# Sigmoid attention and a gated layer on one core: four pairs of 448-token blocks, and the second half of the output layer by seven products

## The chip, the cores and the metric

The kernel runs on one core of one Trainium2 chip. Its time is the device time of one launch in microseconds (us). Before the change the median of three runs is 1235.81 us (1235.44 to 1236.19). A core has a matrix engine (TensorE, "PE" in the profile, with its weight loads shown apart as "PEld"), a vector engine (DVE), a scalar engine (ACT), GpSimd (POOL) and a queue of transfers (SP, "SPq"). Each engine takes its own instructions strictly in the order of the program and waits on semaphores for the others.

## The reference

There are two stages. Sigmoid attention with 8 batches, 12 heads, 448 tokens and a head size of 64, then a gated layer over all 3584 tokens with a model width of 768 and d_ff of 1536:

```
scores = scale * q @ k.T - log(S)
x      = sigmoid(scores) @ v                    # -> 3584 x 768
gate   = sigmoid(x @ w_gate)                    # 768 -> 1536
val    = x @ w_val                              # 768 -> 1536
out    = (gate * val) @ w_out                   # 1536 -> 768
```

q, k and v arrive as 32-bit floats, the three weight matrices as 64-bit floats.

## The kernel before, in words

Attention comes first. It runs over 24 groups of four heads (three groups to a batch) in seven steps each, and it writes x, transposed, to DRAM: six tensors of 128 model rows by 3584 tokens. Beside it, DVE and POOL turn the 64-bit words of the first half of the weights into 32-bit floats (`convert`).

The gated layer works with hidden columns in blocks of 128, taken in pairs `jp`; six pairs in two sets of three. A visit is one set with one group of tokens, and a visit has two parts. In the *units* the hidden values of the three pairs are made: for each pair one unit for the gate (sigmoid on ACT) and one for the value, which is multiplied into the gate. In the *output stage* the hidden values are multiplied with `w_out`. The first set leaves its partial results in DRAM (`part`), the second adds them and writes the result.

Every matrix product is exact to about 32 bits by splitting each operand into a high part (rounded to the format that TensorE takes in one pass) and a low part (the rest). One product of 128x128 weights with a moving tile is thus three matmuls: low weights with high data, high with low, high with high. So every moving tile needs a cast (ACT) and a subtraction (DVE) before it can be used.

A unit works on two hidden blocks times two token blocks at once. It takes seven products in place of eight (Winograd's form of Strassen's scheme), of nine matmuls each: three of the six 128-row slices of x, times three. The sums and differences of the weights are made once by `convert` and lie in DRAM as seven operands (`ad`, loaded into the ring `A` on SP, one per product). The sums of x, in place on POOL, with their casts and low parts are made by `split_x` once per visit. DVE, POOL and ACT add the seven results up to the four blocks (`p1`, `p5`, `u2`, `u3`, `u4`, `c22`, `c`). Work that follows a result is put into a list `later` and is issued after the next product, so that an engine's queue does not stand still for it.

The tokens are seven blocks of 512. Six form three pairs. Block 0 stays alone (`alone`): it takes the ordinary eight block products, two of them per accumulation. The output stage takes the ordinary form throughout: for each of the six output tiles `o` and each token block 18 (first set or second) matmuls, over three pairs, two hidden blocks and three terms; its weights `wo` come through a second ring. The list `visits` sets the order: the first set with block 0 and with the three pairs, then the second set with the last pair, the two others and block 0.

The order in each engine's queue is the order of the Python code. PSUM has eight banks: four for the units (`un`) and four for the output stage (`mm`).

Of the kernel before, what the change touches and what calls it, by code (L numbers as in the profile page):

```python
# [18 lines left out]
P = 128  # L19
# [5 lines left out]
T = 512  # L25

SET = 3
# [7 lines left out]
RING = 6  # L35
RING_OUT = 6
# [3 lines left out]
def sigmoid_attention_glu_kernel(ctx: ExitStack, tc: tile.TileContext, qk, v, wg, wv, wo, out):  # L40
# [22 lines left out]
    NB = B * S // T  # L63
# [9 lines left out]
    N_OPS, A21 = 7, 7  # L73
# [8 lines left out]
    part = [[dram.tile([P, T], F32, name=f"part{b}_{o}") for o in range(NO)] for b in range(NB)]  # L82
    a_dram = [[[dram.tile([P, 2, CW], F32, name=f"ad{jp}_{t}_{n}") for n in range(N_OPS + 1)] for t in range(2)]
              for jp in range(NJ // 2)]
    o_dram = [dram.tile([NO, P, 2, 2, P], F32, name=f"od{jp}") for jp in range(NJ // 2)]


    def chunks(jps):
        res = []
        for jp in jps:  # L90
            for w in (wg, wv, wo):
                res += [w[2 * jp + j][:, c * CW:(c + 1) * CW] for j in range(2) for c in range(2)]
        return res
# [36 lines left out]
    def convert(words, jps):  # L130
# [25 lines left out]
        def to_o(jp, j, c):  # L156
            return lambda hl: [dict(out=o_dram[jp][c * KC:(c + 1) * KC, :, j, n].rearrange("o p f -> p o f"),
                                    in_=hl[:, n].rearrange("p (o f) -> p o f", f=P)) for n in range(2)]

        def chunk(tag, sends):  # L160
            f = pool.tile([P, CW], F32, tag=tag, name="wf", bufs=1)
            words.first(f)
            split(1)
            send(1)
            yield f
            send(0)
            split(0)
            words.second()
            high(f, sends)
            yield f  # L170

        for jp in jps:
            for t in range(2):
                fs = []
                for i, n in enumerate((0, 4, A21, 6)):
                    for f in chunk(f"wf{i}", to_a(jp, t, n)):
                        yield
                    fs.append(f)
                a11, a12, a21, a22 = fs
                split(0)  # L180

                s2 = pool.tile([P, CW], F32, tag="wf4", name="wf", bufs=1)
                for n, (to, x, y, op) in enumerate(((a22, a21, a22, ALU.add), (s2, a22, a11, ALU.subtract),
                                                    (a21, a11, a21, ALU.subtract), (a12, a12, s2, ALU.subtract))):
                    split(1)
                    send(1)
                    nc.gpsimd.tensor_tensor(out=to, in0=x, in1=y, op=op)
                    high(to, to_a(jp, t, (1, 2, 3, 5)[n]))
                    yield
            for j in range(2):  # L190
                for c in range(2):
                    for _ in chunk(f"wf{2 * j + c}", to_o(jp, j, c)):
                        yield
# [6 lines left out]
    SUMS = ("p1", "p5", "u2", "u3", "u4", "c22", "g0", "g1", "g2", "g3", "c0", "c1")  # L200

    def sb(tag):
        return xpool.tile([P, T], F32, tag=tag, name=tag)
# [4 lines left out]
    def load_x(blocks):  # L208

        order = [(i, k) for k in range(KC) for i in range(4)] if len(blocks) == 2 else [(2 * c, k) for c in range(2) for k in range(KC)]  # L210
        for tag, (i, k) in zip(SUMS, order):
            x = sb(tag)
            nc.sync.dma_start(out=x, in_=x_dram[i // 2 * KC + k][:, blocks[i % 2] * T:blocks[i % 2] * T + T])
            xs[i, k] = x
            yield

    def split_x(blocks, cast=nc.scalar.copy):

        sums = {1: (0, 1, 0), 2: (0, 3, 0), 3: (1, 3, 1), 6: (0, 2, 0)} if len(blocks) == 2 else {}
        use = dict(enumerate((0, 0, 0, 1, 2, 3, 0))) if len(blocks) == 2 else {5: 0, 6: 2}  # L220
        for n, i in use.items():
            for k in range(KC):
                if n in sums:
                    to, x, y = sums[n]
                    nc.gpsimd.tensor_tensor(out=xs[to, k], in0=xs[x, k], in1=xs[y, k], op=ALU.subtract)  # L225
                x = xs[i, k]
                hi = xpool.tile([P, T], F32R, tag=f"bh{n}{k}", name="bh")
                lo = xpool.tile([P, T], F32R, tag=f"bl{n}{k}", name="bl")
                cast(hi, x)
                yield  # L230
                nc.vector.tensor_tensor(out=lo, in0=x, in1=hi, op=ALU.subtract)
                bs[n, k] = hi, lo


    wanted = [(jp, t, n) for s, bl in visits for jp in sets[s] for t in range(2)
              for n in (range(N_OPS) if len(bl) == 2 else (0, 4, A21, 6))]
    ring, wos = [], {}

    def load_operand():
        if wanted:  # L240
            jp, t, n = wanted.pop(0)
            ring.append(xpool.tile([P, 2, KC, P], F32R, tag="A", name="A", bufs=RING))
# [12 lines left out]
    with tc.manual_schedule(), tc.tile_pool(name="att", bufs=2) as att, tc.tile_pool(name="sc", bufs=2, space=PSUM) as scp, \  # L255
# [122 lines left out]
        for _ in range(RING_OUT):  # L378
            load_out()
# [241 lines left out]
```

## Time and profile before

| what | us |
|---|---|
| median of three runs | 1235.81 |
| own time of the profiled execution | 1237.49 |
| its span | 1235.3 |
| attention, to the first matmul of the gated layer | 259.3 |
| TensorE busy | 1217.5 |
| DVE, ACT, POOL busy | 658.8, 417.9, 402.2 |

The profile's page shows busy time by engine, the chain of work that ended last, and groups of instructions by line. Rows of the timeline give the start in us from the span's start, the duration in us, the engine, the line, the operation, output and inputs, and in brackets the idle time of the engine just before and what ended it. A matmul's row is longer than the distance to the next one, since matmuls overlap in the array: the distance of starts is what counts. Rows of the windows view give the busy time of each engine in a stretch of time, the granted clock of TensorE as a share of full speed, the share of the 16 DMA engines that was busy, and the rate in GB/s. Rows of the waits view give total us, times and the longest. Rows of the DMA view give the count, KB of one, and the median time from issue to landing.

### The profile page before, as it was taken

The numbers are of one execution on the slowest core, as the hardware profiler recorded it, in microseconds if no ns is written. First come the engines' busy times: TensorE is split into PE (matmuls) and PEld (weight loads), VectorE is DVE, ScalarE is ACT, GpSimd is POOL, SyncE is SP. The second block draws the span as 40 slices with busy tenths as digits, with TensorE's granted clock in tenths as the row PEclk, the third lists the DMA queues.
The fourth block names the chain that finished last, engine by engine and source line by source line (L and its number), as shares of the span: only waits on it lengthen the run. The fifth ranks groups of instructions, "written<-read, shape, count | busy, mean of one in ns | idle before, by whom it ended". The sixth has DMA issues, their size and how long they took to land.

```text
span 1235.3 us, 19057 instructions
## 1 busy us (share of the span) xinstructions
PE 1217.5 (99%) x6916; PEld 902.9 (73%) x6916; DVE 658.8 (53%) x1073; ACT 417.9 (34%) x610; POOL 402.2 (33%) x418
## 2 busy tenths in 40 slices
PE   9999999999799999999999999999999999999998
PEld 3333444468588888887888788888888888888886
DVE  5666677626748867688777601336444452442111
ACT  6777777732312233322412112222222221221010
POOL 2323423304535365534736300235122342220000
PEclk9999999999899999999999999999999999999999
DMA  9999999889699988999788756668766776667745
GB/s 319 327 344 345 357 340 330 296 294 369 228 300 297 281 303 279 299 297 335 259 292 284 231 170 205 193 194 304 233 200 192 267 248 216 194 202 254 226 142 188
DMA packets 150045, 328.43 MB, mean 266 GB/s; under 512 B 15296, under 2 KB 40000, under 8 KB 149952
## 3 DMA queue, kind: packets, MB, share of 16 engines
q1 hardware_dynamic: 149952, 327.22, 79.4%
q8 instruction: 55, 0.90, 0.3%
q14 instruction: 38, 0.31, 0.1%
HBM read 246.94 MB, written 80.22 MB: 265 GB/s over the span
## 4 chain that ended last, share of the span: by engine, by line
PE 93%; DMA 3%; DVE 2%; POOL 1%; ACT 0%; issue 0%; SPq 0%; POOLq 0%; DVEq 0%; ACTq 0%
PE un L401 42%; PE acc L503 26%; PE sc L279 9%; PE av L296 9%; PE un L461 7%; DMA ad<-whl 1%; DMA A<-ad 1%; DMA xd<-x 0%; DVE hl L485 0%; DMA wo<-od 0%; PE sc L334 0%; DVE whl L140 0%; POOL g L225 0%; DVE wf L126 0%; DVE x L313 0%
## 5 line engine op out<-in xcount | busy, mean ns | idle before, releaser
L401 PE MATMUL un<-bh,A 128*128 128x512 f32 x1512 | 466.4, 389 | 0.0
L401 PEld LDWEIGHTS un<-bh,A 128*128 128x128 f32 x1512 | 283.8, 188 | 58.7
L503 PE MATMUL acc<-hh,wo 128*128 128x512 f32 x1008 | 314.4, 391 | 1.6 <-DMA wo<-od 1.0
L401 PE MATMUL un<-bl,A 128*128 128x512 f32 x756 | 294.1, 389 | 0.0
L503 PEld LDWEIGHTS acc<-hh,wo 128*128 128x128 f32 x1008 | 190.1, 189 | 43.2 <-DMA wo<-od 2.1
L503 PE MATMUL acc<-hl,wo 128*128 128x512 f32 x504 | 197.6, 392 | 8.7 <-DVE hl L485 8.7
L282 ACT ACTIVATE a<-sc,bias 128x896 f32<-128x896 f32 x168 | 169.2, 1008 | 67.0 <-PE sc L279 63.3
L401 PEld LDWEIGHTS un<-bl,A 128*128 128x128 f32 x756 | 141.9, 188 | 29.6
L279 PE MATMUL sc<-qk 64*64 64x448 f32 x1344 | 159.7, 541 | 0.5 <-ACT a L282 0.5
L296 PE MATMUL av<-a,v 64*64 64x448 f32 x1344 | 158.3, 536 | 0.0
L150 POOL CAST whl<-wf 128x384 fp32r<-128x384 f32 x120 | 72.5, 605 | 263.4 <-DVE wf L128 209.2
L414 POOL TENSOR_TENSOR u<-u,p 128x512 f32<-128x512 f32 x36 | 47.7, 1325 | 274.9 <-DVE u L414 274.5
L503 PEld LDWEIGHTS acc<-hl,wo 128*128 128x128 f32 x504 | 95.0, 189 | 30.3 <-DVE hl L485 10.7
L279 PEld LDWEIGHTS sc<-qk 64*64 64x64 f32 x1344 | 55.7, 134 | 73.4 <-issue 60.1
L414 DVE TENSOR_TENSOR u<-un,p 128x512 f32<-128x512 f32 x36 | 24.8, 689 | 157.1 <-PE un L401 157.1
L296 PEld LDWEIGHTS av<-a,v 64*64 64x64 f32 x1344 | 55.6, 133 | 70.7 <-issue 70.1
L484 ACT CAST hh<-g 128x512 fp32r<-128x512 f32 x72 | 42.2, 621 | 191.2 <-DVE g L481 142.7
L448 ACT ACTIVATE g<-c 128x512 f32<-128x512 f32 x72 | 43.1, 628 | 153.1 <-DVE c L414 149.0
L461 PE MATMUL un<-bh,A 128*128 128x512 f32 x288 | 89.4, 390 | 1.8 <-DMA A<-ad 1.8
L140 DVE TENSOR_TENSOR whl<-wf,whl 128x384 fp32r<-128x384 f32 x120 | 82.6, 692 | 8.3 <-POOL whl L150 8.2
L414 DVE TENSOR_TENSOR ob<-acc,pb 128x512 f32<-128x512 f32 x42 | 29.0, 691 | 93.3 <-PE acc L503 88.2
L115 POOL TENSOR_SCALAR wf<-wf 128x384 f32<-128x384 f32 x72 | 43.5, 604 | 84.5 <-DVE wf L114 52.8
(53 smaller groups left out, 1128.7 us busy)
## 6 DMA issues: line engine op xcount, KB each, us to landing
A<-ad SPq DMA_DIRECT2D x300, 384.0 KB, 3.8
ad<-whl SPq DMA_DIRECT2D x96, 384.0 KB, 5.8
wo<-od SPq DMA_DIRECT2D x144, 256.0 KB, 4.0
qk<-qk SPq DMA_DIRECT2D x23, 896.0 KB, 6.9
v<-vv SPq DMA_DIRECT2D x24, 448.0 KB, 6.1
xd<-x SPq DMA_DIRECT2D x48, 224.0 KB, 5.9
part<-ob SPq DMA_DIRECT2D x42, 256.0 KB, 3.5
pb<-part SPq DMA_DIRECT2D x42, 256.0 KB, 3.8
```

What stands on the lines that cost most here:

```text
L115: nc.gpsimd.tensor_scalar(out=f, in0=f, scalar1=F32_MAX, scalar2=F64_ZERO, op0=ALU.min, op1=ALU.max)
L140: nc.vector.tensor_tensor(out=hl[:, 1], in0=to, in1=hl[:, 0], op=ALU.subtract)
L150: nc.gpsimd.tensor_copy(hl[:, 0], to)
L279: nc.tensor.matmul(sc[halves[u], h, :S], lhsT=qkt[halves[h], p, k0:k0 + HP], rhs=qkt[halves[h], p, :S], start=True, stop=True)
L282: nc.scalar.activation(a, sc[:, :, :S], AF.Sigmoid, bias=bias, scale=scale)
L296: nc.tensor.matmul(avs[key][halves[h], :S], lhsT=vt[halves[u], g, h], rhs=a[halves[u], h], start=start, stop=g == last)
L401: nc.tensor.matmul(acc, lhsT=w, rhs=m, start=i == 0, stop=i == len(terms) - 1)
L414: engine.tensor_tensor(out=to, in0=x, in1=y, op=ALU.add)
L448: nc.scalar.activation(gates[i], acc, AF.Sigmoid)
L461: nc.tensor.matmul(acc, lhsT=w, rhs=m, start=i == 0, stop=i == len(terms) - 1)
L484: nc.scalar.copy(hh, g)
L503: nc.tensor.matmul(acc, lhsT=w, rhs=m, start=i == 0 and some[0] == 0, stop=i == len(terms) - 1 and some[-1] == SET - 1)
```

## The change

Tokens are now eight blocks of 448, one batch each, in four pairs; `alone` is gone, and every unit uses the seven products. There are eight visits: the first set with pairs 0 to 3, then the second set with pairs 3, 0, 1, 2. The x of pair 0 is loaded and split during attention, for seven operands of three slices (before: the two halves of block 0, six slices), by POOL casts.

In the second set, the output stage takes the seven products too. The "weights" are then a pair of output tiles (`o` and `o + 3`) by a pair of hidden blocks, the moving side is a pair of hidden blocks by a pair of token blocks, and the three pairs `jp` of the set are added in PSUM: three pairs times three terms, nine matmuls to a product. The sums of `w_out` are made by `convert` (`oo` in DRAM; 36 steps to a pair in place of 32) and come through the same ring `A`. The sums, casts and low parts of the hidden values are made in `hidden_operands`. The partial results of the first set are added on POOL (`partial`). The units and output products of the second set share eight PSUM banks (`us`).

Besides, the last two of the three terms of a product trade places (high weights with high data comes before high weights with low data), `split_x` issues sum, cast and low part of one slice in three successive steps, a corner of the weights that no product uses is not written to DRAM any more, and both rings have eight places in place of six.

```diff
-    pairs = [(b, b + 1) for b in range(1, NB, 2)]
-    visits = [(0, bl) for bl in [(0,)] + pairs] + [(1, bl) for bl in pairs[-1:] + pairs[:-1] + [(0,)]]
+    pairs = list(range(B // 2))
+    visits = [(0, pr) for pr in pairs] + [(1, pr) for pr in pairs[-1:] + pairs[:-1]]
...
+    def product(pool, operands, dims="p (a k f) -> p a k f"):
+
+        acc = pool.tile([P, 512], F32, tag="un", name="un")[:, :S]
+        a = ring.pop(0).rearrange(dims, a=2, f=P)
+        terms = []
+        for k, (hi, lo) in enumerate(operands):
+            w = (a[:, 0, k], a[:, 1, k]) if dims.startswith("p (a") else (a[:, k, 0], a[:, k, 1])
+            terms += [(w[1], hi), (w[0], hi), (w[0], lo)]
...
+    with tc.manual_schedule(), tc.tile_pool(name="fs", bufs=1, reuse_waits="tile") as fs, \
+            tc.tile_pool(name="us", bufs=8, space=PSUM, reuse_waits="tile") as us:
...
+        def hidden_operands(slot):
...
+            def value(i, acc):
+                gated(i, acc)
+                b[i] = gates[i]
+                if i == 0:
+                    high(0)
+                    later.append(lambda: low(0))
+                elif i == 3:
+                    later.append(lambda: (high(5), later.append(lambda: low(5))))
+                elif i == 1:
+                    total(1)
+                    total(3)
+                    later.append(lambda: (high(1), low(1), high(3), low(3), total(2)))
+                else:
+                    high(4)
+                    later.append(lambda: (high(2), low(2), low(4), total(6), later.append(lambda: (high(6), low(6)))))
...
+            def step():
+                nonlocal steps
+                steps += 1
+                send_due(steps)
+                for _ in range(2):
+                    next(x_loads, None)
+                if steps > 2:
+                    next(splits, None)
+                if steps % 4 == 0:
+                    next(splits, None)
+
+            for o in range(KC):
...
+                nc.scalar.copy(p1, out_product(0))
+                nc.scalar.copy(p5, out_product(1))
+                plus(u2, out_product(2), p1)
+                plus(u4, u2, p5, nc.gpsimd)
+                partial(p1, p1, 0, 0)
+                partial(u4, u4, 0, 1)
+                plus(u3, out_product(3), u2)
+                plus(p5, u3, p5, nc.gpsimd)
+                ob = result()
+                partial(ob, p5, 1, 1)
+                partial(u3, u3, 1, 0)
+                send(1, 1, ob, 3)
+                for n, x, m, t in ((4, p1, 0, 0), (5, u4, 0, 1), (6, u3, 1, 0)):
+                    ob = result()
+                    plus(ob, out_product(n), x)
+                    send(m, t, ob)
+                load_part(o + 1)
```

How the change moves instructions is shown at the first output stage of the second set, for DVE first. In the rows, `g0` to `g3` are the four blocks gate times value of the last pair, `hh` and `hl` their high and low parts, `c0` and `c1` sums out of PSUM, `ou`, `op` and `ob` tiles of the output stage; the numbers tell buffers apart. Before, from the last unit's fifth product on:

```order
L414 TENSOR_TENSOR c1_9515<-un_9516,p1_9455 128x512
L481 TENSOR_TENSOR g0_9419<-c1_9515,g0_9419 128x512
L485 TENSOR_TENSOR hl_9530<-g0_9419,hh_9529 128x512
L414 TENSOR_TENSOR c0_9533<-un_9534,u4_9459 128x512
L414 TENSOR_TENSOR c1_9554<-un_9555,u3_9458 128x512
L481 TENSOR_TENSOR g2_9453<-c1_9554,g2_9453 128x512
L485 TENSOR_TENSOR hl_9548<-g3_9434,hh_9547 128x512
L485 TENSOR_TENSOR hl_9552<-g1_9437,hh_9551 128x512
L485 TENSOR_TENSOR hl_9571<-g2_9453,hh_9570 128x512
L414 TENSOR_TENSOR ob_9633<-acc_9598,pb_8877 128x512
```

And with the change, from the same product on:

```order
L408 TENSOR_TENSOR c1_9019<-un_9020,p1_8959 128x448
L465 TENSOR_TENSOR g0_8923<-c1_9019,g0_8923 128x448
L225 TENSOR_TENSOR hl_9035<-g0_8923,hh_9034 128x448
L408 TENSOR_TENSOR c0_9037<-un_9038,u4_8963 128x448
L225 TENSOR_TENSOR hl_9073<-g0_8923,hh_9072 128x448
L225 TENSOR_TENSOR hl_9077<-g1_8941,hh_9076 128x448
L408 TENSOR_TENSOR c1_9056<-un_9057,u3_8962 128x448
L465 TENSOR_TENSOR g2_8957<-c1_9056,g2_8957 128x448
L225 TENSOR_TENSOR hl_9070<-g3_8938,hh_9069 128x448
L225 TENSOR_TENSOR hl_9105<-g0_8923,hh_9104 128x448
L225 TENSOR_TENSOR hl_9084<-g2_8957,hh_9083 128x448
L225 TENSOR_TENSOR hl_9128<-g0_8923,hh_9127 128x448
```

There are seven low parts in place of four, and two of them (of `g0` and `g1` after the first sums) stand ahead of the sum of the unit's last product, `c1_9056`.

On ACT, at the same place, before:

```order
L484 CAST hh_9529<-g0_9419 128x512
L484 CAST hh_9547<-g3_9434 128x512
L484 CAST hh_9551<-g1_9437 128x512
L484 CAST hh_9570<-g2_9453 128x512
L229 CAST bh_9637<-p1_9574 128x512
```

And with the change:

```order
L584 CAST hh_9034<-g0_8923 128x448
L584 CAST hh_9069<-g3_8938 128x448
L584 CAST hh_9072<-g0_8923 128x448
L584 CAST hh_9076<-g1_8941 128x448
L584 CAST hh_9083<-g2_8957 128x448
L584 CAST hh_9104<-g0_8923 128x448
L664 COPY op1_9086<-un_9091 128x448
L584 CAST hh_9127<-g0_8923 128x448
```

The high part of the third operand, `hh_9104`, stands behind that of `g2`, `hh_9083`.

On POOL, from the last unit's fourth product on, before:

```order
L414 TENSOR_TENSOR c22_9460<-u3_9458,p5_9456 128x512
L481 TENSOR_TENSOR g3_9434<-c22_9460,g3_9434 128x512
L481 TENSOR_TENSOR g1_9437<-c0_9533,g1_9437 128x512
L225 TENSOR_TENSOR p1_9574<-p5_9576,p1_9574 128x512
L225 TENSOR_TENSOR u4_9582<-c22_9584,u4_9582 128x512
```

And with the change:

```order
L408 TENSOR_TENSOR c22_8964<-u3_8962,p5_8960 128x448
L465 TENSOR_TENSOR g3_8938<-c22_8964,g3_8938 128x448
L465 TENSOR_TENSOR g1_8941<-c0_9037,g1_8941 128x448
L225 TENSOR_TENSOR g0_8923<-g1_8941,g0_8923 128x448
L225 TENSOR_TENSOR g1_8941<-g3_8938,g1_8941 128x448
L225 TENSOR_TENSOR g0_8923<-g3_8938,g0_8923 128x448
L225 TENSOR_TENSOR g0_8923<-g2_8957,g0_8923 128x448
L408 TENSOR_TENSOR ou4_9090<-ou2_9088,op5_9087 128x448
L408 TENSOR_TENSOR op1_9086<-op1_9086,pb_8345 128x448
L408 TENSOR_TENSOR ou4_9090<-ou4_9090,pb_8347 128x448
L408 TENSOR_TENSOR op5_9087<-ou3_9089,op5_9087 128x448
L408 TENSOR_TENSOR ob_9181<-op5_9087,pb_8351 128x448
```

Four sums of the hidden values come in, and the six sums of each output step; the sums of the next pair's x (`p1_9574<-p5_9576,p1_9574` before) come behind them.

More of the change, by code (lines that the diff above doesn't have):

```diff
@@ L377, in sigmoid_attention_glu_kernel, with after, run_later, plus @@
             pass
-        for _ in range(RING_OUT):
-            load_out()
+    later = []
+    def after():
+        for f in list(later):
+            later.remove(f)
+            f()
+    def run_later():
+        while later:
+            later.pop(0)()
+    def plus(to, x, y, engine=nc.vector):
+        engine.tensor_tensor(out=to, in0=x, in1=y, op=ALU.add)
+    cs = itertools.cycle(("c0", "c1"))
+    def product(pool, operands, dims="p (a k f) -> p a k f"):
[5 more added lines that the diff above has]
+            terms += [(w[1], hi), (w[0], hi), (w[0], lo)]
+        for i, (w, m) in enumerate(terms):
+            nc.tensor.matmul(acc, lhsT=w, rhs=m, start=i == 0, stop=i == len(terms) - 1)
+        load_operand()
+        after()
+        return acc
+    def unit(pool, tick, done):
+        def next_product(n):
+            return product(pool, [bs[n, k] for k in range(KC)])
+        p1, p5, u2, u3, u4, c22 = (sb(n) for n in SUMS[:6])
+        nc.scalar.copy(p1, next_product(0))
+        tick()
+        nc.scalar.copy(p5, next_product(1))
+        tick()
+        plus(u2, next_product(2), p1)
+        plus(u4, u2, p5, nc.gpsimd)
+        tick()
+        plus(u3, next_product(3), u2)
+        plus(c22, u3, p5, nc.gpsimd)
+        tick()
+        c = sb(next(cs))
+        plus(c, next_product(4), p1)
+        done(0, c)
+        later.append(lambda: done(3, c22))
+        tick()
+        c = sb(next(cs))
+        plus(c, next_product(5), u4)
+        done(1, c)
+        tick()
+        c = sb(next(cs))
+        plus(c, next_product(6), u3)
+        done(2, c)
+        tick()
+    gates = {}
+    def gate(i, acc):
+        gates[i] = sb(f"g{i}")
+        nc.scalar.activation(gates[i], acc, AF.Sigmoid)
+    def gated(i, acc):
+        engine = nc.vector if i in (0, 2) else nc.gpsimd
+        engine.tensor_tensor(out=gates[i], in0=acc, in1=gates[i], op=ALU.mult)
+        return engine
     with tc.manual_schedule(), tc.tile_pool(name="ff", bufs=1, reuse_waits="tile") as ff, \
@@ L468, in gate_alone, with load_out @@
-        def gate_alone(i, acc):
-            gates[i] = ff.tile([P, T], F32, tag="ob", name="ob", bufs=3)
-            nc.scalar.activation(gates[i], acc, AF.Sigmoid)
-        def hidden(slot, products):
+        wanted_out = [(jp, o) for _ in pairs for o in range(NO) for jp in sets[0]]
+        def load_out():
+            if wanted_out:
+                jp, o = wanted_out.pop(0)
+                wos[jp, o] = ff.tile([P, 2, 2, P], F32R, tag="wo", name="wo", bufs=RING_OUT)
+                nc.sync.dma_start(out=wos[jp, o].bitcast(F32), in_=o_dram[jp][o])
@@ L474, in hidden @@
+        for _ in range(RING_OUT):
+            load_out()
+        def hidden(slot, tick):
             hs = {}
             def value(i, acc):
-                g = gates[i]
-                hh = ff.tile([P, T], F32R, tag=f"hh{slot}{i}", name="hh")
-                hl = ff.tile([P, T], F32R, tag=f"hl{slot}{i}", name="hl")
-                engine = nc.vector if products is alone or i in (0, 2) else nc.gpsimd
-                engine.tensor_tensor(out=g, in0=acc, in1=g, op=ALU.mult)
+                engine = gated(i, acc)
+                hs[i] = tuple(ff.tile([P, S], F32R, tag=f"h{a}{slot}{i}", name=f"h{a}") for a in "hl")
```

351 lines of the change are left out of this document (159 added, 192 removed).

## The prediction

> **What bounds the kernel now.** I read the busy times first, then the chain of waits, then TensorE's own waits. Page and chain:
>
> ```profile
> span 1235.3 us, 19057 instructions
> PE 1217.5 (99%) x6916; PEld 902.9 (73%) x6916; DVE 658.8 (53%) x1073; ACT 417.9 (34%) x610; POOL 402.2 (33%) x418
> PE 93%; DMA 3%; DVE 2%; POOL 1%; ACT 0%; issue 0%; SPq 0%; POOLq 0%; DVEq 0%; ACTq 0%
> 257.05 2.25 PE av L296 x24
> 259.30 7.93 PE un L461 x34
> 752.70 85.68 PE un L401 x378
> 838.38 49.01 PE acc L503 x216
> 1218.89 12.55 PE acc L503 x54
> ```
>
> TensorE is busy for 99% of the span and makes 93% of the chain. The gated layer starts at 259.3 and its matmuls end at 1218.89 + 12.55 = 1231.4. The chain's unbroken pieces give the price of one matmul, start to start: 85.68 / 378 = 0.2267 us, and 49.01 / 216 the same. The groups by line give the count (a row of high data each; the low data make half as many again):
>
> ```profile
> L401 PE MATMUL un<-bh,A 128*128 128x512 f32 x1512 | 466.4, 389 | 0.0
> L503 PE MATMUL acc<-hh,wo 128*128 128x512 f32 x1008 | 314.4, 391 | 1.6 <-DMA wo<-od 1.0 <-ACT hh L484 0.5
> L461 PE MATMUL un<-bh,A 128*128 128x512 f32 x288 | 89.4, 390 | 1.8 <-DMA A<-ad 1.8
> ```
>
> 1.5 x (1512 + 1008 + 288) = 4212 matmuls, times 0.2267 = 954.9 us. So the profiled span is 259.3 + 954.9 + 17.2 of waits and slow clock + 3.9 after the last matmul = 1235.3. The median of the runs, 1235.81, is 0.5 above this span. TensorE's waits:
>
> ```profile
> PE acc L503 <- DVE hl L485: 8.7, 4, 4.9
> PE un L461 <- DMA A<-ad: 1.8, 1, 1.8
> PE acc L503 <- DMA wo<-od: 1.0, 1, 1.0
> 324.53 0.80 PE L503 MATMUL acc<-hl,wo 128*128 128x512 f32 x1 [4.94 <-DVE hl L485]
> 326.40 1.06 PE L503 MATMUL acc<-hh,wo 128*128 128x512 f32 x2
> 327.25 0.63 PE L503 MATMUL acc<-hl,wo 128*128 128x512 f32 x1
> ```
>
> Nearly all are output stages that start before the low parts of the last hidden values are there; and after the 4.94 us wait matmuls stand (327.25 - 326.40) / 2 = 0.425 us apart, at half the clock.
>
> **The matmuls.** Now all up products go by sevens: 4 pairs x 6 hidden pairs x 2 x 7 x 9 = 3024. The first set's output: 8 blocks x 6 tiles x 18 = 864. The second set's: 4 pairs x 3 x 7 x 9 = 756. In sum 4644 in place of 4212, each with 448 columns in place of 512. Columns fall from 2,156,544 to 2,080,512, by 3.5%. What matters is whether a 448-column matmul really is shorter. Streaming 512 columns at half the clock takes 0.425 us, so about 0.213 at the full clock, and some 0.0133 of the 0.2267 is overhead. If it is fixed, 448 columns take 0.1867 + 0.0133 = 0.2000; if all is in proportion, 0.1983. From the other side the weight load could forbid any gain, 0.2267. These rows tell how near that is:
>
> ```profile
> 332.31 0.19 PEld L503 LDWEIGHTS acc<-hh,wo 128*128 128x128 f32 x1 [0.33 <-DMA wo<-od]
> 332.42 0.19 PEld L503 LDWEIGHTS acc<-hl,wo 128*128 128x128 f32 x1
> 332.65 0.42 PEld L503 LDWEIGHTS acc<-hh,wo 128*128 128x128 f32 x2
> ```
>
> A load takes 0.19 us in the records, but after a wait the next one starts 0.11 later: the array has taken the first by then. 0.11 is well under 0.20, and even 0.19 is. I take 0.2000: 4644 x 0.2000 = 928.8 us, 26.1 less.
>
> The Trainium skill, "TensorE: Matmul & The Clock Gate", section "Back-to-back issue gap", gives N / 2.4 GHz plus 2.5 ns. That is 216 ns for 512 columns where this trace has 227, so its constant is too small here; with the constant taken as fixed, its sum would fall by the same 26.7 ns per matmul.
>
> **Attention.** It loses six slices of early splitting and gains 21, with 12 sums on POOL.
>
> ```profile
> 0.00:259.30 259.30, 257.40 (x2705) 112.09 (x2705) 162.82 (x330) 190.19 (x216) 83.03 (x130) 1.00 0.94 328
> ```
>
> DVE (162.8 of 259.3) and POOL (83.0) have room for some 10 and 22 us more; ACT, which feeds TensorE here, gets nothing. Nothing in this stage moves: 0. If DVE came late with the sums that free the PSUM tiles of `av`, the price would be a few us; that is in the range.
>
> **First set, four output stages.** The 4.9 us wait came from the early splits of the next pair, pushed through at the end of the first visit; they are gone. The three others together had 8.7 - 4.9 = 3.8. The cover before the third hidden pair's terms is 24 matmuls, now 4.8 us in place of 5.4, while `convert`'s steps (108 in place of 96 over a shorter time) keep their length in the same queue. I take 3.8 / 3 = 1.25 for each of four: 5 us (0 to 8).
>
> **Second set, four output stages: a new wait.** This is how such a transition runs now; DVE and POOL from the timeline, ACT's cast from the groups:
>
> ```profile
> 969.02 0.69 DVE L414 TENSOR_TENSOR c<-un,p 128x512 f32<-128x512 f32 x1 [1.29 <-PE un L401]
> 969.75 1.26 DVE L481 TENSOR_TENSOR g<-c,g 128x512 f32<-128x512 f32 x1
> 971.69 0.69 DVE L485 TENSOR_TENSOR hl<-g,hh 128x512 fp32r<-128x512 f32 x1 [0.69 <-ACT hh L484]
> 972.30 1.49 DVE L414 TENSOR_TENSOR c<-un,u 128x512 f32<-128x512 f32 x2
> 973.83 1.08 DVE L481 TENSOR_TENSOR g<-c,g 128x512 f32<-128x512 f32 x1
> 973.07 1.29 POOL L481 TENSOR_TENSOR g<-c,g 128x512 f32<-128x512 f32 x1 [2.60 <-DVE c L414]
> L484 ACT CAST hh<-g 128x512 fp32r<-128x512 f32 x72 | 42.2, 621 | 191.2 <-DVE g L481 142.7
> ```
>
> The output stage began at 973.07, just when POOL could start block `g1`. With 7/8 of the columns I use 1.13 for POOL, 0.60 for DVE (0.95 where it writes `g`), 0.55 for a cast, and count from the start of the output stage. POOL: `g1` to 1.1, first sum to 2.3, second to 3.4. ACT: cast of the first sum to 2.8; DVE: its low part to 3.4 or 3.5. ACT: cast of the second to 3.95; DVE: its low part to 4.6. Only then comes the sum of the unit's last product on DVE, to 5.2, and block `g2`, to 6.1. POOL's third sum is done at about 4.8, but its cast stands on ACT behind that of `g2`: 6.1 + 0.55, then 0.55, is 7.2, and its low part is there at 7.8. TensorE wants these in the third product, after 2 x 9 matmuls and six more: 4.8 for the high part, 5.2 for the low. It waits 2.4 and then 0.2: 2.6 us. The second product needs its parts at 3.0 and 3.4, and has them at 2.8 and 3.5; the later ones are in time. Four visits: 10.4 us. Below, POOL and DVE run unhindered in another order of events and it is 6; above, with DVE and POOL slowed by each other, 3.5 each and half clock behind it, 18. Behind the waiting matmul stand all others; only the PSUM results that DVE still owes gain time.
>
> **Second set, the rest of its output stages.** Each lasts 21 x 1.8 = 37.8 us, and three of four also load and split the next pair. Three things could run late:
>
> ```profile
> A<-ad SPq DMA_DIRECT2D x300, 384.0 KB, 3.8
> 285.00:300.00 15.00, 15.00 (x68) 12.43 (x67) 9.32 (x17) 3.40 (x6) 3.44 (x4) 1.00 1.04 402
> L225 POOL TENSOR_TENSOR g<-c,g 128x512 f32<-128x512 f32 x15 | 22.5, 1498 | 1.3 <-DVE bl L231 1.3
> 994.94 1.75 POOL L225 TENSOR_TENSOR g<-c,g 128x512 f32<-128x512 f32 x1
> 995.46 1.78 DVE L231 TENSOR_TENSOR bl<-g,bh 128x512 fp32r<-128x512 f32 x1
> ```
>
> Transfers: 21 operands of 393 kB and 32 tiles of 229 kB are 15.6 MB, 413 GB/s, and the queues have moved 402. They end 1 us late, and the ring runs eight products, 14.4 us, ahead of a latency of 3.8. POOL: 18 sums of results and 12 of x are 30 x 1.13 = 34 us, or 39 at 1498 x 7/8 = 1.31 us, for 37.8 + 2.6. Nine of the sums of x fall into the middle third, where POOL gets some 5 us late. SP then waits for POOL's result ahead of the next loads, and DVE with it. Eight PSUM banks (14.4 us) and the ring cover that. I take 1 us in all; uncovered it is some 5 us in each of three stages.
>
> The last visit has no next pair. Behind its last matmul stand as before one DVE sum and one transfer: 3.9. The first operands come with two more places in the ring and without the early loads of x beside them: 0.5 in place of 1.8.
>
> **Sum.** 259.3 + 928.8 + (0.5 + 5 + 10.4 + 1 = 16.9) + 3.9 = 1208.9, and 0.5 to the median: 1209 us. The gain is nearly all columns; the waits come out as long as before, in other places.
>
> **The rivals.**
>
> *A matmul does not get shorter with its columns* (slower). If the loads of weights, 0.19 us in every record, need more than the 0.20 us between starts, spacing stops falling. The point from which this decides is (1235.3 - 259.3 - 3.9 - 16.9) / 4644 = 0.2057 us. With no gain at all, 4644 x 0.2267 = 1052.8 and the time is 1333; half way, 0.2133, it is 1271. For it: all matmuls of this shape in the trace have 512 columns, so no row shows a shorter one. Against it: 0.11 between loads after the wait. 0.10.
>
> *POOL becomes the bound of the output stages.* The last two rows above overlap and both last far longer than the 1.29 and 0.69 of others like them: POOL and DVE hinder each other when both read two tiles of SBUF. If POOL's 30 sums and DVE's 21 low parts went one after another, 34 + 21 x 0.60 = 46.6 us, 6 over 40.4. Three stages: 18 us, 1227. Against it: eight banks and the ring give more than 6 us of cover, and the x splits may end within the next units. 0.12. The Trainium skill, "SBUF — State Buffer", section "Who interferes with whom", has this as an exclusive lock: a DVE instruction with two SBUF inputs and a GpSimd one that reads SBUF go one after the other. The two rows agree in kind (1.75 and 1.78).
>
> *Everything hides:* 0.1983 a matmul (920.9) and half the waits, 8.4: 259.3 + 920.9 + 8.4 + 3.9 + 0.5 = 1193. 0.10.
>
> **How the numbers follow.** The forecast has 0.68, with a range of its own of 1195 to 1222 (the waits' bounds, and 0.1983). The range for 8 in 10 takes in part of the two rivals at its ends: 1192 to 1232. A difference of 0.2%, 2.5 us, is about what can be told from none. Faster by more: forecast, "everything hides" and most of "POOL", 0.86. Within it: 0.03, the edge of POOL and a spacing close to 0.2057. Slower: 0.11, the first rival and a remainder.
>
> **What would show it.** In the new profile: pieces of 378 matmuls in the chain of 75.6 us (0.2000); attention's end at 259 to 260; in TensorE's waits four of 2 to 3 us on the cast or the low part of the hidden values, in the third product of each of the second set's output stages; POOL near full there; no wait for operands after the first visit. The forecast is wrong if spacing is over 0.203, if TensorE waits for PSUM, x or operands in the second set, or if attention ends later than 262.

## The result and the profile after

The change made the kernel slower: 1268.34 us (1267.35 to 1268.98) against 1236.0 beside it, a ratio of 1.0261 (95% interval 1.0243 to 1.0279). The forecast was 1209, with a range that ended at 1232. The profiled execution took 1267.97 us with a span of 1266.2. Its page, the engines' shares of the chain, and TensorE's waits:

```profile
span 1266.2 us, 20742 instructions
PE 1221.4 (96%) x7348; PEld 992.0 (78%) x7348; DVE 778.3 (61%) x1226; ACT 459.5 (36%) x739; POOL 623.9 (49%) x622
PE 78%; POOL 7%; DMA 5%; DVE 5%; issue 3%; ACT 1%; SPq 1%; POOLq 0%; DVEq 0%
PE un L421 <- DMA A<-ad: 14.1, 5, 4.5
PE un L421 <- ACT hh L584: 9.1, 4, 2.3
PE un L421 <- DVE ob L408: 6.3, 3, 3.5
PE un L421 <- POOL wf L114: 3.6, 1, 3.6
PE acc L514 <- DVE hl L225: 2.8, 4, 1.3
```

TensorE's share of the chain fell from 93 to 78%, and in place of four late low parts it now waits for operands (`A<-ad`), for casts of hidden values (`hh`), for PSUM tiles that DVE had to read (`ob`) and for a step on a weight (`wf`). The pieces of the chain show the spacing, which isn't one number:

```profile
389.75 78.13 PE un L421 x378
512.95 71.15 PE un L421 x351
```

That is 78.13 / 378 = 0.2067 us and 71.15 / 351 = 0.2027. Between two waits the spacing stays at one of these two values; some seven in ten matmuls stand at the lower one, and the mean is 0.2039. The forecast of the prediction used 0.2000.

From the distances between successive starts of matmuls, counted over all of the gated layer, the two spans divide like this (half clock: distances of 0.30 to 0.44 us, less one ordinary spacing; waits: distances over 0.44, less the same; some short stalls fall under half clock too):

| us | before | forecast | after |
|---|---|---|---|
| attention, to the gated layer's first matmul | 259.2 | 259.3 | 259.0 |
| matmuls at their ordinary spacing | 4212 x 0.2268 = 955.3 | 4644 x 0.2000 = 928.8 | 4644 x 0.2039 = 947.0 |
| half clock | 3.0 | with the waits | 12.2 |
| waits | 13.7 | 16.9 | 44.0 |
| from the last matmul's start to the end | 4.3 | 3.9 | 4.3 |

The miss of 57 us is 18 us of spacing and 39 of waits with the half clock behind them. By place, the waits are 5.3 us at the start of the gated layer, 3.5 in the first set's output stages, 12.2 at the head of the second set's four output stages, and 23 in the rest of these stages and the units behind them. Of the 12.2 us of half clock 5.4 lie in this last place, 4.1 at the heads of the output stages and 2.3 at the start of the gated layer.

**The new wait at the head of the second set's output stages** came as drawn up. ACT, DVE and PE rows of the first of them:

```profile
837.91 0.63 DVE L465 TENSOR_TENSOR g<-c,g 128x448 f32<-128x448 f32 x1
838.57 1.03 ACT L584 CAST hh<-g 128x448 fp32r<-128x448 f32 x2 [2.82 <-DVE g L465]
837.01 0.37 PE L421 MATMUL un<-hl,A 128*128 128x448 f32 x1
839.65 0.66 PE L421 MATMUL un<-hh,A 128*128 128x448 f32 x2 [2.27 <-ACT hh L584]
```

The two casts run back to back: that of `g2`, just made on DVE, and behind it the third operand's, for which TensorE stands from 837.0 to 839.65. The stage began at 831.3, so the part was there at 8.3 us and was wanted at 5.9.

**The rest of the stage.** These are two rows of POOL at the end of a stretch without a pause, then windows of the same stage (columns: us, then busy time and instructions of PE, PEld, DVE, ACT and POOL, granted clock, share of the DMA engines, GB/s), then SP's queue, and what TensorE did:

```profile
867.70 1.42 POOL L408 TENSOR_TENSOR ob<-op,pb 128x448 f32<-128x448 f32 x1
871.29 1.15 POOL L225 TENSOR_TENSOR p<-g,p 128x448 f32<-128x448 f32 x1
```

```profile
843.70:872.40 28.70, 28.69 (x139) 25.72 (x137) 15.44 (x19) 6.97 (x15) 28.50 (x22) 1.00 0.79 293
864.00:870.00 6.00, 6.00 (x31) 5.45 (x30) 1.50 (x2) 0.57 (x1) 5.92 (x6) 1.00 0.18 70
882.00:888.00 6.00, 6.00 (x20) 5.39 (x21) 1.18 (x2) 1.40 (x3) 5.06 (x5) 0.63 0.97 384
```

```profile
861.26 0.32 SPq L267 DMA_DIRECT2D A<-ad  x1
869.14 4.67 SPq L634 DMA_DIRECT2D y<-ob  x3
873.87 1.87 SPq L621 DMA_DIRECT2D pb<-part  x4
875.84 0.38 SPq L267 DMA_DIRECT2D A<-ad  x1
SPq L634 <- POOL ob L408: 44.8, 11, 8.1
```

```profile
877.06 0.36 PE L421 MATMUL un<-bl,A 128*128 128x448 f32 x1
881.89 1.09 PE L421 MATMUL un<-bh,A 128*128 128x448 f32 x2 [4.47 <-DMA A<-ad]
```

POOL works through 22 sums in 28.7 us without a pause. SP has reached the sending of a result (`y<-ob`) that POOL hasn't made: POOL ends it at 869.1. SP issues nothing from 861.6 to 869.1, the transfers die down (0.18 of the DMA engines from 864 to 870), and the next operand for the units is issued at 875.84, because three results and four partial tiles stand ahead of it too. TensorE has used up its ring by 877.1 and waits to 881.9, and then it runs at half clock for a while (a granted clock of 0.63 from 882 to 888). In the next two visits TensorE waits for operands in the same place, and in the third also 5.2 us for PSUM tiles that DVE had to read.

**The start of the gated layer.** DVE, POOL and PE:

```profile
272.69 0.36 DVE L113 TENSOR_SCALAR wf<-wraw 128x384 uint32<-128x384 uint32 x1 [12.00 <-DMA wraw<-wg]
273.24 0.62 DVE L408 TENSOR_TENSOR u<-un,p 128x448 f32<-128x448 f32 x1
270.00 0.37 PE L421 MATMUL un<-bl,A 128*128 128x448 f32 x1
273.96 0.65 PE L421 MATMUL un<-bh,A 128*128 128x448 f32 x2 [3.59 <-POOL wf L114]
```

DVE waits 12 us for raw weight words (`wraw`), whose load is issued behind eight loads of `wo`. Behind that step in DVE's queue stands the first sum that reads a PSUM tile of the units; TensorE stops when its four tiles are full. Before, the same step waited nearly as long:

```profile
271.61 0.36 DVE L114 TENSOR_SCALAR wf<-wraw 128x384 uint32<-128x384 uint32 x1 [10.63 <-DMA wraw<-wg]
```

It held up no matmul there: in the first visit's ordinary products (`alone`) a PSUM tile takes 18 matmuls, and with the change it takes nine.

### The profile page after: what moved, and what is told of

Its sections match the earlier page's. It is cut to its first block, busy times and chain, and to the rows that moved or that the text cites. A ratio compares the mean times of both kernels' runs of the same rounds, so it can differ in the third digit from the quotient of the medians.

```text
span 1266.2 us, 20742 instructions
## 1 busy us (share of the span) xinstructions
PE 1221.4 (96%) x7348; PEld 992.0 (78%) x7348; DVE 778.3 (61%) x1226; ACT 459.5 (36%) x739; POOL 623.9 (49%) x622
## 4 chain that ended last, share of the span: by engine, by line
PE 78%; POOL 7%; DMA 5%; DVE 5%; issue 3%; ACT 1%; SPq 1%; POOLq 0%; DVEq 0%
PE un L421 47%; PE acc L514 12%; PE sc L295 10%; PE av L312 10%; DMA A<-ad 2%; POOL ou L408 1%; DVE hl L225 1%; DMA y<-ob 1%; POOL u L225 1%; POOL p L225 1%; POOL op L408 1%; POOL g L225 1%; POOL g L465 1%; DMA qk<-qk 1%; DVE g L465 1%
## 5 line engine op out<-in xcount | busy, mean ns | idle before, releaser
L421 PE MATMUL un<-bh,A 128*128 128x448 f32 x2016 | 581.3, 370 | 22.1 <-DMA A<-ad 14.1
L421 PEld LDWEIGHTS un<-bh,A 128*128 128x128 f32 x2016 | 382.7, 190 | 58.5 <-issue 12.6
L421 PE MATMUL un<-bl,A 128*128 128x448 f32 x1008 | 372.1, 369 | 0.0
L514 PE MATMUL acc<-hh,wo 128*128 128x448 f32 x576 | 164.7, 366 | 0.0
L421 PE MATMUL un<-hh,A 128*128 128x448 f32 x504 | 145.9, 371 | 12.1 <-ACT hh L584 9.1
L225 DVE TENSOR_TENSOR hl<-g,hh 128x448 fp32r<-128x448 f32 x132 | 101.5, 791 | 78.2 <-ACT hh L584 72.1
L514 PEld LDWEIGHTS acc<-hh,wo 128*128 128x128 f32 x576 | 108.2, 188 | 9.1
L421 PEld LDWEIGHTS un<-hh,A 128*128 128x128 f32 x504 | 94.8, 190 | 23.7 <-ACT hh L584 12.1
L514 PE MATMUL acc<-hl,wo 128*128 128x448 f32 x288 | 105.8, 367 | 2.8 <-DVE hl L225 2.8
L421 PE MATMUL un<-hl,A 128*128 128x448 f32 x252 | 93.9, 373 | 1.7 <-DVE hl L225 1.7
```

The costliest lines, as they stand in the source:

```text
L225: engine.tensor_tensor(out=to, in0=x, in1=y, op=ALU.subtract)
L421: nc.tensor.matmul(acc, lhsT=w, rhs=m, start=i == 0, stop=i == len(terms) - 1)
L514: nc.tensor.matmul(acc, lhsT=w, rhs=m, start=i == 0 and some[0] == 0, stop=i == len(terms) - 1 and some[-1] == SET - 1)
```

## The experiments

Ratios are against the kernel before, timed beside each run.

### What a matmul of fewer columns costs

The first kernel leaves out all of the reference's work and runs only matmuls with 128x128 weights that change with each:

```diff
+SWEEP = ((512, 512), (480, 512), (448, 512), (448, 448), (416, 448), (384, 384), (320, 320), (256, 256), (128, 128))
+        for rep in range(3):
+            for n, width in (SWEEP if rep % 2 == 0 else SWEEP[::-1]):
+                for group in range(10):
+                    acc = ps.tile([P, 512], F32, tag="acc", name=f"acc{n}of{width}")[:, :n]
+                    for i in range(9):
+                        nc.tensor.matmul(acc, lhsT=ws[i], rhs=mv[width, (i + group) % 6][:, :n], start=i == 0, stop=i == 8)
```

> Nothing but TensorE: groups of nine 128x128 matmuls in a row, 90 for each number of columns, three times over, and none of the reference's work. In the changed kernel the distance of two starts at 448 columns was 0.2027 or 0.2067 us, in place of the forecast 0.2000. Theory, an overhead beside the columns that is between 0.013 and 0.020 us: 512 columns 0.2267, 480 0.213 to 0.220, 448 0.200 to 0.207, 416 0.187 to 0.194, 384 0.173 to 0.180, 320 0.147 to 0.153, 256 0.120 to 0.127. Rival, the load of the weights is a floor: everything from 448 columns down stands at 0.20 to 0.207. A third way, the place of the tiles: 448 columns cut from tiles of 512 differ from tiles of 448.

Its rows for TensorE, each a run of matmuls of one width:

```profile
153.90 20.21 PE L61 MATMUL acc128of<-m,w 128*128 128x128 f32 x180
173.95 6.33 PE L61 MATMUL acc256of<-m,w 128*128 128x256 f32 x51
230.55 36.65 PE L61 MATMUL acc448of<-m,w 128*128 128x448 f32 x180
267.04 19.66 PE L61 MATMUL acc480of<-m,w 128*128 128x480 f32 x90
286.54 19.68 PE L61 MATMUL acc512of<-m,w 128*128 128x512 f32 x86
```

From start to start, 128 columns take 20.05 / 180 = 0.1114 us, 448 take 36.49 / 180 = 0.2027, and 480 take 19.50 / 90 = 0.2167. The weight load isn't the limit at 448: spacing goes on falling, to about 0.111, as much as the 0.11 between loads that the prediction had read. The place of the tiles does nothing: 448 columns cut from tiles of 512 and tiles of 448 have the same 0.2027. But 448 isn't at 0.2000 either. A second kernel, again with nothing of the reference's work, put a wait ahead of each block of 90 matmuls and took widths on both sides of 448:

```diff
+WIDTHS = (512, 496, 464, 456, 448, 440, 432, 400)
+        for segment in range(5):
+            for n in WIDTHS if segment % 2 == 0 else WIDTHS[::-1]:
+                if res is not None:
+                    ws[0] = sb.tile([P, P], F32R, tag="late", name="late", bufs=2)
+                    for _ in range(3):
+                        nc.scalar.copy(res[:, :400], res[:, :400])
+                    nc.scalar.copy(ws[0], res[:, :P])
```

> Only TensorE, and none of the reference's work: blocks of 90 matmuls of 512, 496, 464, 456, 448, 440, 432 and 400 columns, five blocks of each width, and ahead of each block a wait of TensorE for a chain of copies on ACT (some 2 to 3 us). The changed kernel's 448-column matmuls stood 0.2027 us apart in some stretches and 0.2067 in others. Theory: the state is set by the restart behind each wait, so every block of 448 is at one of these two values from start to end, with blocks of both among the five, and the 512-column blocks are all at 0.2268. Rival: the spacing is a function of the columns alone, and what differed in the kernel was the other engines' work: all five 448-column blocks then have one value, 0.2027, as nothing else runs here. On the columns: if the 16 to 17 ns over columns / 2.4 seen at 448 and 480 are a step above some width, 432 and 440 stand at 13.3 over it (0.1933, 0.1967) and 456 to 496 at 16 or more.

Two blocks of 448 columns; between the first and second row of each pair lie five whole groups of nine matmuls:

```profile
468.67 1.78 PE L65 MATMUL acc448of<-m,w 128*128 128x448 f32 x8
477.79 1.78 PE L65 MATMUL acc448of<-m,w 128*128 128x448 f32 x8
828.76 1.81 PE L65 MATMUL acc448of<-m,w 128*128 128x448 f32 x8
838.06 1.81 PE L65 MATMUL acc448of<-m,w 128*128 128x448 f32 x8
```

(477.79 - 468.67) / 45 = 0.2027, and (838.06 - 828.76) / 45 = 0.2067. Four of the five blocks of 448 are at the first value from the end of the half clock to their last matmul, one at the second, and the only other work is ACT's copies. So the theory held on its main point: the state is set at the restart, and a stretch keeps it. A restart isn't the only thing that can change a spacing: in the first kernel, which has no such waits, 416 columns took 186.7 ns where they followed 448 and 188.3 where they followed 384. What decides between the two values stays open. All widths, worked out in the same way (from two kernels, 256 to 384, 416 and 480 from the first). The time of the columns alone is reckoned at 2.4 columns to a ns, which these runs give too: (512 - 400) / (226.7 - 180.0) = 2.4.

| columns | spacing, ns | ns over columns / 2.4 | ns per column |
|---|---|---|---|
| 256 | 120 | 13.3 | 0.469 |
| 384 | 173.5 | 13.5 | 0.452 |
| 400 | 180.0 | 13.3 | 0.450 |
| 416 | 186.7 to 188.3 | 13.4 to 15.0 | 0.449 to 0.453 |
| 432 | 195.8 | 15.8 | 0.453 |
| 440 | 200.0 | 16.7 | 0.455 |
| 448 | 202.7 or 206.7 | 16.0 or 20.0 | 0.452 or 0.461 |
| 456 | 208.9 | 18.9 | 0.458 |
| 464 | 208.9 or 210.0 | 15.6 or 16.7 | 0.450 or 0.453 |
| 480 | 216.7 | 16.7 | 0.451 |
| 496 | 223.4 | 16.7 | 0.450 |
| 512 | 226.7 | 13.3 | 0.443 |

The second guess, that 432 and 440 still stand at 13.3 over the streaming time, missed: they don't, and there is no step between two widths but a bulge from 416 to 496. Of the widths tried, 512 is the cheapest per column, and 448 is among the dearest from 400 up.

### Four pairs of 448 alone

This kernel keeps the pairs of 448 and gives the second set the ordinary output layer back, 4752 matmuls in all:

```diff
-            if s:
-                break
             js = sets[s]
+            if s:
+                load_part(*tiles[0])
+                load_part(*tiles[1])
...
-                nc.scalar.copy(ob, acc)
+                if s:
+                    plus(ob, acc, pbs.pop((t, o)))
+                else:
+                    nc.scalar.copy(ob, acc)
```

> Four pairs of 448-token blocks with the output layer in the ordinary form in both sets: 3024 + 1728 = 4752 matmuls. With the 0.2039 us a matmul of the changed kernel: 259 + 969 + waits of about 16 + 4 = 1248 us, so this half of the change already loses some 12 us. If a matmul took the forecast 0.2000, it would be 1230.

Measured: 1241.09 us (1235.49 to 1248.12), ratio 1.0031 (1.0006 to 1.0055). The profiled run was the slowest, 1248.12. Two pieces of its chain:

```profile
385.94 76.61 PE un L415 x378
627.55 78.14 PE un L415 x378
```

76.61 / 378 = 0.2027 up to some 590 us, 78.14 / 378 = 0.2067 from there to the end. TensorE's waits list one of 4.1 us and one of 1.0 in the gated layer, so here nearly all is spacing: with 0.2000 it was to be 1230. The expected 1248 had 16 us of waits in it; by the starts they and the half clock are 8.2 in all. The two spacings can also account for the 13 us between this kernel's runs, where the 19 of before lie within 7: 4752 x 0.0040 = 19 us lie between all matmuls at one and all at the other. Only one of the runs has a trace, so this isn't shown. The first part of the change, by itself, gains nothing (0.3% slower), and the seven products of the output layer cost the other 27 us.

### The x sums off POOL

In the second set's output stages DVE makes the next pair's 12 sums of x in place of POOL; transfers, their order and their number stay:

```diff
-    def split_x(cast=nc.scalar.copy):
+    def split_x(cast=nc.scalar.copy, adder=nc.gpsimd):
...
-                    subtract(nc.gpsimd, *sums[n])
+                    subtract(adder, *sums[n])
...
-            splits = split_x() if nxt else iter(())
+            splits = split_x(adder=nc.vector) if nxt else iter(())
```

> The changed kernel with the twelve sums of the next pair's x on DVE in place of POOL, in the output stages of the second set alone. Theory, POOL is full there, its late results hold up the SP queue, and the operands queued behind come late: POOL loses 12 of 30 sums, the waits for operands and for PSUM in and after these stages (about 23 us, and some 9 of half clock) go, and the time falls to 1236 to 1245. Rival, the 413 GB/s that these stages ask of the transfers are the limit: the waits stay, 1262 to 1270.

Measured: 1244.05 us (1239.48 to 1247.49), ratio 1.0055 (1.0037 to 1.0073). Its waits for operands and for POOL's results, and the window that had died down:

```profile
PE un L421 <- DMA A<-ad: 1.2, 2, 0.8
SPq L634 <- POOL ob L408: 35.1, 12, 7.9
864.00:870.00 6.00, 6.00 (x31) 5.46 (x30) 5.00 (x10) 1.16 (x4) 1.99 (x2) 1.00 0.71 224
```

24 us come back, as expected, with TensorE's wait for operands down from 14.1 to 1.2 and that for `ob` gone. SP still waits 35.1 us for POOL in all, but at the place of the first stage it stands from 860.1 to 863.5 in place of 861.6 to 869.1, and that much the ring covers. POOL's load was the source, and the transfers were not.

### SP's queue

Two kernels leave POOL its work and change what SP meets. The first loads the partial tiles a step ahead and sends results three or four products later:

```diff
-                        pbs[m, t, o] = fs.tile([P, S], F32, tag=f"pb{m}{t}", name="pb")
+                        pbs[m, t, o] = fs.tile([P, S], F32, tag=f"pb{m}{t}", name="pb", bufs=2)
...
-                send(1, 1, ob, 3)
+                send(1, 1, ob, 6)
...
-                    send(m, t, ob)
-                load_part(o + 1)
-            send_due(steps + 3)
+                    send(m, t, ob, 5)
+            send_due(steps + 9)
```

> The changed kernel with POOL's work as it is, but nothing on SP that waits for POOL in the second set's output stages: results are sent two to four products later, partial results are loaded one step earlier into a second set of buffers. Theory, SP's queue is the way on which POOL's lateness reaches TensorE: the waits for operands (14 us and the half clock behind them) go, 1243 to 1255. Rival, POOL's lateness reaches TensorE through PSUM all the same: 1260 to 1270.

Measured: 1278.1 us (1275.04 to 1281.07), ratio 1.0329 (1.03 to 1.0358): slower still, and outside both expectations. The edit did not do what it was meant to. SP's rows and TensorE's at the end of the first such stage:

```profile
874.82 0.99 SPq L267 DMA_DIRECT2D A<-ad  x2
884.93 4.86 SPq L636 DMA_DIRECT2D y<-ob  x4
893.74 4.33 SPq L267 DMA_DIRECT2D A<-ad  x8
899.31 1.08 PE L421 MATMUL un<-bh,A 128*128 128x448 f32 x2 [7.21 <-DMA A<-ad]
```

All results that are left are sent at the stage's end, ahead of the next visit's operands, and SP stands there from 875.8 to 884.9. It moved the wait to a worse place: a longer wait of SP is a longer wait of TensorE. The second kernel sends the last results during the next units and loads the partial tiles there:

```diff
         def no_tick():
-            pass
+            nonlocal steps
+            steps += 1
+            send_due(steps)
...
-            load_part(0)
             for slot in range(SET):
                 unit(us, no_tick, gate)
                 hidden_operands(slot)
+                if slot < 2:
+                    load_part(slot)
...
-            send_due(steps + 3)
```

> In sp_free the results that were left at the end of an output stage all went out ahead of the next visit's operands, and SP still stood 9.1 us there for POOL. Here they go out between the next unit's products, and partial results are loaded during the units; POOL's work is as in the changed kernel. Theory, SP's queue is the way on which POOL's lateness reaches TensorE: SP waits for POOL under 5 us in all ahead of operands, TensorE's waits for operands go from 14.1 to under 2 us, 1243 to 1255. Rival, what POOL owes holds up PSUM as well: waits for DVE's and ACT's results take their place, 1258 to 1270.

Measured: 1249.42 us (1246.41 to 1250.51), ratio 1.0097 (1.0082 to 1.0113), inside the expected range and 19 us under the change with POOL's work untouched. TensorE no longer waits for operands at all. Two rows of what is left, SP's and TensorE's:

```profile
SPq L578 <- POOL ob L408: 13.7, 8, 3.4
PE un L421 <- ACT p L432: 4.4, 3, 1.6
```

POOL is as late as with the change, and TensorE meets it only for these 4.4 us, just behind three stages: there ACT, which is to empty a PSUM tile, stands behind a cast of a sum that POOL makes late. By the starts, the 23 us of waits in the rest of the stages are down to some 5. So most of POOL's lateness cost time because SP's one queue carried it to the operand loads. The half clock stays at 11.8 us in all, in another place: all four waits for the cast are now followed by some, where with the change one was.

### The order of the casts

```diff
-                    high(4)
-                    later.append(lambda: (high(2), low(2), low(4), total(6), later.append(lambda: (high(6), low(6)))))
+                    later.append(lambda: (high(2), low(2), high(4), low(4), total(6), later.append(lambda: (high(6), low(6)))))
```

> The changed kernel with one cast moved in ACT's queue: the high part of the third operand (hi2) stands ahead of that of g2 in place of behind it. Theory as predicted, the wait in the third product of each of the second set's output stages (2.64 us from start to start, four times) comes from this place in the queue: hi2 is ready at about 5.4 us in place of 7.2, the wait falls to 1 us or less, and the time by 6 to 9 us, to 1258 to 1263. Rival, the low part or POOL's third sum is as late: the wait stays over 2 us and the time at 1266 to 1270.

Measured: 1262.12 us (1257.94 to 1264.92), ratio 1.0201 (1.0182 to 1.022). The wait for the cast (9.1 us) is gone from the list, and there is another in its place:

```profile
PE un L421 <- DVE hl L225: 7.7, 8, 1.5
```

The low part of the same operand is late on DVE, behind the last product's sum and the block `g2`. The time came out in the expected range by luck: from start to start the wait in the third product fell from 2.44 to 1.94 us, not to 1, and the four heads together have 2.0 us less of waits, but 1.3 more of half clock. Most of the 5.6 us between the two profiled spans lies elsewhere: 3.7 of waits in the rest of these stages and the units behind them, with no reason shown. The rival had the low part right, and the wait just under its 2 us.

### All together

The third kernel takes the x sums on DVE, this order of casts, and raw words of the second set's weights loaded ahead of the eight `wo` tiles; the fourth adds the sending and loading of the second SP kernel:

```diff
-        for _ in range(RING_OUT):
-            load_out()
...
         words = Words(ff, chunks(sets[1]), AHEAD_FF, 4)
+        for _ in range(RING_OUT):
+            load_out()
```

> The changed kernel with three edits: sums of x on DVE (as in x_sums_dve, 1244), the cast's place (as in high_order), and the first weights of the second set loaded ahead of the output weights in SP's queue at the start of the gated layer (the wait of 4 to 5 us at 274 us). If the three are independent: 1244 - 8 - 6 = 1230, 0.5% faster than before. Rival, the spacing of 0.2027 or 0.2067 leaves no gain: 1234 to 1240.

> The three edits and SP's freed queue of sp_free_2. If SP's waits for POOL still cost something once POOL has less to do, 1 to 4 us under three_mends; if not, the same within 2 us.

Measured: three 1234.68 us (1230.93 to 1238.18), ratio 0.9985 (0.9972 to 0.9998); four 1230.73 us (1226.79 to 1232.01), ratio 0.9944 (0.9929 to 0.9959). The third lies where the rival had it, and not at 1230. The fourth is 4.0 us under it, as much as expected, but their profiled runs differ by 5.6 us of spacing and only 1.7 of waits and half clock, so how much of the 4.0 is SP's isn't shown. The fourth beats both kernels, by 0.6% and by 3%. Its profiled span is 1229.9 us, and of its waits:

```profile
PE un L421 <- DVE hl L225: 7.7, 8, 1.5
SPq L577 <- POOL ob L408: 2.8, 2, 1.8
```

In the same division as above: 259.6 of attention, 4644 x 0.2034 = 944.7, half clock 5.9, waits 15.5, and 4.2. With waits near those of before, the gain is the matmuls' 955.3 - 944.7 = 10.6 us, less 4.7 of waits and half clock. An estimate from these figures: without any wait it would be 259.0 + 4644 x 0.2027 + 4.3 = 1204.6 us of span in the one state and 1223.2 in the other, where before would be at 259.2 + 955.3 + 4.3 = 1218.8.

## Why the prediction was wrong

**"I take 0.2000" (the matmuls): wrong by 18 us.** The reasoning was right in kind: there is a fixed part beside the streaming, the weight load is no floor, and the rival "a matmul does not get shorter with its columns" is refuted by the spacings of 0.180 at 400 columns and 0.111 at 128. But the fixed part was read off 512 columns alone, one of the widths at which it is least, and was taken to be the same at 448. There it is 16 or 20 ns in place of 13.3. The prediction gave all that lies above 0.2000 to one rival, tied to the weight load, with a chance of 0.10; a fixed part that changes with the width was not among its cases. The stated condition for failing, a spacing over 0.203, came true with the mean of 0.2039.

**"Second set, the rest of its output stages ... I take 1 us": wrong, 23 us of waits and 5.4 of half clock.** POOL's lateness was foreseen ("nine of the sums of x fall into the middle third, where POOL gets some 5 us late"), and so was the first step of the chain ("SP then waits for POOL's result ahead of the next loads"). What failed is the sentence behind it, that eight banks and the ring cover this. A ring of eight covers 14 us of latency only if its loads are issued on time; SP issues them, and SP stood up to 8.1 us, then had three results and four partial tiles to issue as well. The cover was counted as if the queue that fills it were free. The two SP kernels show it: with the queue freed the wait for operands goes from 14.1 to 0, with the wait at the stage's end it becomes 22.1. Even the prediction's price for the uncovered case, some 5 us in each of three stages, was too small against 23: it counted POOL's lateness, and not what SP then still had to issue ahead of the operands. The rival "POOL becomes the bound of the output stages" had the right source and 18 us, but not the way: 30 sums at the measured 1.30 us are 38.9, under the 40.4 of a stage, and at 872.4 POOL stood idle again. It was late in the middle of the stage, and SP's queue carried that on. With the queue freed, 4.4 us of waits were left.

**"First operands ... 0.5 in place of 1.8": wrong, 5.3.** Only the ring and the loads of x were looked at. The first visit's units are now seven products, whose sums on DVE free a PSUM tile after every nine matmuls, and the first of them stands behind a DVE step that waits for raw weight words. The two more loads of `wo` ahead of these words count for some 1 us (272.69 against 271.61). The kernel with the pairs alone has the same wait, 4.1 us. Loading the words first, in the third kernel, took it away, and left 1.9 us for an operand, as before the change: so the 0.5 for that wait was too low as well.

**What held.** Attention is where it was (259.0), with DVE at 183.4 and POOL at 108.7 busy, so the extra splitting was hidden, though it gave DVE 20.6 us more in place of some 10:

```profile
0.00:259.02 259.02, 256.92 (x2705) 114.00 (x2705) 183.43 (x339) 190.22 (x216) 108.68 (x151) 1.00 0.95 327
```

"First set, four output stages: 5 us" was 3.5. "A new wait: 2.6 us" in each of four visits was 2.64 and 0.80 between starts more than a spacing of 0.2 each, some 3.05 a visit and 12.2 in all against 10.4. The larger is the third product's wait for the cast, 2.44 against 2.4: the place, the engine and the order of events came as worked out from the order of instructions and the rows. That the size is so close is in part luck, since both ends came 1.1 us late (8.3 and 5.9 us into the stage, in place of 7.2 and 4.8). The smaller is the low part of the second product's operand, 0.60 where the prediction had 0.1. What it did not see there is that freeing ACT alone leaves DVE as the next wait. The tail was 4.3 for 3.9.

The sum of these differences, 18.2 + 22 + 12.2 + 4.8 + 1.8 - 1.5 - 0.3 + 0.4 = 57.6, is the distance from 1208.9 to the span of 1266.2, within the rounding.

## What to carry to other kernels

A price taken from one size of an instruction is a guess for another, even one 12% smaller: leave room between the proportional value and the limit, and try the size by itself before a whole kernel is cut to it. A buffer ring covers lateness only while the queue that fills it runs; where a store waits for a late engine in the same queue as the loads, that engine's lateness can reach the consumer through a ring that is deep enough for the loads' own latency, so such stores belong behind the loads of what comes next. When a late instruction is moved forward in one queue, follow its operand through the next engine's queue too: here the cast came early and the low part on DVE was late next.

## What was not expected of the hardware

- **Two spacings for the same matmul.** At 448 columns 0.2027 or 0.2067 us, set anew by a restart after a wait and then kept for hundreds of matmuls. The Trainium skill, "TensorE: Matmul & The Clock Gate", section "Back-to-back issue gap", gives columns / 2.4 GHz plus 2.5 ns as the gap of a single matmul at the full clock. In these runs, where every matmul has a weight load of its own, 13.3 ns is the least that comes on top, and it isn't the same for all widths.
- **The same wait, with and without the half clock.** Two waits of the second spacing kernel:

```profile
844.40 0.47 PE L65 MATMUL acc440of<-m,late 128*128 128x440 f32 x1 [2.67 <-ACT late L61]
844.71 1.56 PE L65 MATMUL acc440of<-m,w 128*128 128x440 f32 x7
887.43 0.70 PE L65 MATMUL acc400of<-m,late 128*128 128x400 f32 x1 [2.66 <-ACT late L61]
887.93 2.80 PE L65 MATMUL acc400of<-m,w 128*128 128x400 f32 x8
```

  Behind the first, matmuls go on at 0.20 us, behind the second eight take 0.33 each. Of 39 such waits of 3.0 to 3.1 us from start to start, 25 were followed by 7 to 11 matmuls at half clock and 14 by at most one. So in this kernel a wait near 3 us costs its length, and in two of three cases 1 to 2 us on top (7 to 11 matmuls, 0.15 to 0.2 us each).
- **POOL beside DVE.** The changed kernel's sums on POOL took 1.15 us in some rows and 1.42 and more in others of the same shape. From 830 us on, the 107 that ran beside no DVE instruction with two SBUF inputs (or for under 0.1 us) took 1.15 in the mean, the other 96 took 1.34. The 22 of the unbroken stretch took 28.5, so 30 would take 38.9: the prediction's upper bound of 39, and not the 34 that its 1 us rested on.
